# Threshold searches with TENSOR_TENSOR alone on GpSimd, looks over 583 columns, and searches in batches 2 to 5

## The chip, the cores and the metric

The kernel runs on one core of a Trainium2 chip. The metric is the device time of one execution in microseconds; smaller is better. The core's engines are named as in the profile: PE (matrix products), PEld (its weight loads), DVE (vector engine), ACT (scalar engine), POOL (GpSimd) and SP (which issues DMAs).

## The reference

Two stages follow each other: attention in which each query keeps its 32 largest scores, and a two-layer network with a squared ReLU.

```python
# q, k, v: (8 batches, 8 heads, 576 rows, 64), float32
scores = scale * np.matmul(q, k.transpose(0, 1, 3, 2))
kth = np.partition(scores, -32, axis=-1)[..., -32:-31]
scores = np.where(scores >= kth, scores, -1000000000.0)
scores = scores - np.max(scores, axis=-1, keepdims=True)
attn = np.exp(scores)
attn = attn / (np.sum(attn, axis=-1, keepdims=True) + 1e-09)
attn_out = np.matmul(attn, v)
# x: attn_out as (4608, 512); w_in (512, 2048), w_out (2048, 512)
h = x @ w_in
r = np.maximum(h, 0.0)
out = (r * r) @ w_out
```

## The kernel before

**Groups.** The 64 heads form 32 pairs. A group is 128 query rows of both heads of a pair, so a row of SBUF holds 2 x 576 scores. A pair has four and a half groups; the half ones (the last 64 rows, `Z` in the code) of two pairs make one group. That gives 144 groups, 18 in each batch.

**A usual group** (`top_k`, L820). PE makes the scores in PSUM, ACT copies them to a tile `s` (L752; there are five). The 32nd largest score of each row is then found on DVE: folds in PSUM make a quarter-size array of maxima (L890), POOL adds and subtracts scores as integers, which leaves the smaller partners (L885: two kinds of `u`, then `f`), and DVE takes the eight largest and strikes them out, in turn (L919, L924, L928, L931). With the threshold `kth`, ACT makes a mask `w` (L950, two instructions), PE transposes scores and mask, ACT takes the exponential (L1006), and PE multiplies with the values. Chunks of finished rows go through the network: ReLU on ACT (L1125), squares on POOL (L1137) or ACT (L1140), output copies on ACT (L1157), stores from SP.

**A hunted group.** Four groups find their threshold another way (`hunt`, L756, with `hunted`, L812, for the mask), with ACT and POOL in place of DVE. ACT copies the scores to the one tile `hs`. Then ACT *looks* at them six times, two instructions each (`look`, L766), into the one tile `hz`, with a sum per row as a by-product. The first look gives the sum of squares, from which POOL makes a first threshold (a scaling, then a power of 1/2, L778 and L779). Each of the next four looks takes the sign of threshold minus score; the sum tells how many scores lie above. POOL corrects the threshold in four small operations on two columns (`tiny`, L784 to L789): it rounds the count's distance from its aim to a multiple of 16 by adding and taking off a large constant (`ROUND`), multiplies by a gain and by the first threshold, and adds. The sixth look gives signs and a final count. POOL multiplies signs and scores (L793), so that the scores below the threshold are the largest, DVE takes their eight largest (L795), and POOL selects by the count which of the eight is the 32nd (L797, L799; `hot` holds the eight counts). DVE brings it into `hth` (L800). POOL compares it with 0 and with the last threshold and writes into `fcmp` (L803 to L807).

**Flag and second pass.** At the end (`verdict`, L1361) DVE reduces all comparisons of `fcmp` to one flag. If it is set, the program computes everything again with full searches on DVE. In the profiled execution it was not.

**Order of work.** There is no order by hand. Each operation is handed to a planner (`Plan.op`, L109) with an engine, an estimated duration, a priority and its dependencies; `Plan.schedule` (L141) runs the whole program through these estimates, takes on each engine the ready operation with the smallest priority, and what comes out is the fixed order on each engine's queue. On the chip, semaphores keep dependencies, and a queue waits in order. A group's priorities are counted from `tg = T0 + PER * (number of groups before)`, with PER = 5.3. In a search, look `j` has priority `tg + HO + HS * j`, its POOL operations `tg + HS * j - 14`, the two maxima `tg + HD`. HO, HS, HD are constants (L448), and `HA`, `HP`, `HZ` are estimates of durations.

**Where searches lie.** `HUNT` (L465) names the hunted groups, by batch, head pair and group, and how many groups earlier the search begins: `{(2, 2, 3): 12, (3, 2, 3): 12, (4, 2, 3): 12, (6, 2, 3): 12}`. In batches 5 and 6 the two half groups come first; in batch 6 the groups are ordered by rows ahead of head pairs, in batches 1 to 5 by head pairs.

**Setup.** `setup` (L1306) writes constants, with POOL's `hot` columns among them (L1323, L1324).

Of the kernel before, what the change touches and what calls it, by code (L numbers as in the profile page):

```python
# [6 lines left out]
ALU = mybir.AluOpType  # L7
ACTF = mybir.ActivationFunctionType
AX = mybir.AxisListType
FP32 = mybir.dt.float32  # L10
# [3 lines left out]
P = 128  # L14
TOPK = 32
NEG = -3.0e38
# [368 lines left out]
def bass_top_k_attn__then__act_relu_squared_kernel(  # L385
# [71 lines left out]
    NGRP = NALL // 2  # L457
    NF = 3
    GAP = QUART + NGRP // NF + 8
# [11 lines left out]
    hk = sb("hk", [P, NH, 2 * (NSTEP + 1) + 8 * NSTEP + 2 + 2 + 32 + 4])  # L471
# [9 lines left out]
    sizes = {  # L481
        "rq": ([P, 5, 2, D], FP32, 3), "rk": ([P, 5, 2, D], FP32, 2), "rv": ([P, 10, D], FP32, 2),
        "qk": ([P, 2 * S + 64], FP32, 5), "vb": ([P, 10, D + 1], BF16, 5),
        "s": ([P, 2 * S + 4], FP32, 5), "hs": ([P, 2, S], FP32, 1), "hz": ([P, 2 * S + 4], FP32, 1), "u": ([P, 2 * (HALF + QUART) + 4], FP32, 1), "f": ([P, 2, 2 * GAP + S + NGRP // NF], FP32, NF), "a": ([P, 2, 8], FP32, 2),
        "sh": ([P, 2], FP32, 2), "w": ([P, 2, S], BF16, 3), "p": ([P, 9, 128], BF16, 3),
        "av": ([P, 10, D + 1], FP32, 2), "x": ([P, 10, D], BF16, 3), "xt": ([P, NCT, 256], BF16, 3),
        "xz": ([P, NCT, 64 * 2], BF16, 2), "o": ([P, DM], FP32, 2),
# [1 line left out]
    mem = {nm: sb(nm, *spec) for nm, spec in sizes.items()}  # L489
# [17 lines left out]

    def at(t):
        x = mem[t.pool.name][t.slot]
        if t.pool.name == "hz":  # L510
            return x[:, 2:2 + 2 * S].rearrange("p (i c) -> p i c", i=2)
# [16 lines left out]
    act, vec, gp, pe = nc.scalar, nc.vector, nc.gpsimd, nc.tensor  # L528
# [57 lines left out]
    def build(full, weights, pl):  # L586
        state = {"h": 0, "n": 0, "u": 0, "pairs": 0, "last": {}}
        kths, rzs, checks, sought = [], [], [], {}
# [167 lines left out]
        def hunt(k, gi, qks, tg):  # L756

            st, hz = tile("hs"), tile("hz")
            score(gi, qks, tg, st)
            used = [0]  # L760

            def small(n_):
                used[0] += n_
                return lambda a=0, b=n_, c=used[0] - n_: hk[:, k, c + a:c + b]

            def look(j, func, acc, after, bias=None):  # L766
                kw = [dict() if bias is None else dict(bias=bias(i, i + 1), scale=-1.0) for i in range(2)]
                return [pl.op("act", HA - .09 * (j == 0), tg + HO + HS * j + .1 * i, lambda i=i: act.activation(  # L768
                    at(hz)[:, i, :], at(st)[:, i, :], func, accum_out=acc(i, i + 1), **kw[i]), r=[st], after=after,
                    w=[hz] if j == 0 else [], hold=[] if j == 0 else [hz], take=[hz] if j == i == 0 else [])  # L770
                    for i in range(2)]
# [4 lines left out]
            q, t0 = small(2), small(2)  # L776
# [3 lines left out]
            t = t0  # L780
            for j in range(NSTEP):
                a, r, v, m, t_ = small(2), small(2), small(2), small(2), small(2)
                got = look(j + 1, ACTF.Sign, a, got, t)
                got = tiny(j + 1, lambda a=a, r=r: gp.tensor_scalar(  # L784
                    r(), a(), 27.5 * 2 - S, ROUND, ALU.add, ALU.add), got)
                got = tiny(j + 1, lambda r=r, v=v, j=j: gp.tensor_scalar(
                    v(), r(), ROUND, -GAIN[j] / START / 2, ALU.subtract, ALU.mult), got)
                got = tiny(j + 1, lambda v=v, m=m: gp.tensor_tensor(m(), v(), t0(), ALU.mult), got, .155)
                got = tiny(j + 1, lambda t=t, m=m, t_=t_: gp.tensor_tensor(t_(), t(), m(), ALU.add), got, .155)  # L789
                t = t_  # L790
            a, z8, pick = small(2), small(16), small(16)
            got = look(NSTEP + 1, ACTF.Sign, a, got, t)
            z = pl.op("gp", HZ, tg + HS * (NSTEP + 1) - 14, lambda: gp.tensor_tensor(  # L793
                at(hz)[:, :, :], at(hz)[:, :, :], at(st)[:, :, :], ALU.mult), r=[st], hold=[hz], after=got)
            mx = [pl.op("dve", .065 + S / 960, tg + HD, lambda i=i: vec.max(z8(8 * i, 8 * i + 8), at(hz)[:, i, :]),  # L795
                        hold=[hz], after=[z]) for i in range(2)]
            which = [pl.op("gp", .26, tg + HS * (NSTEP + 1) - 13, lambda i=i: gp.tensor_scalar(  # L797
                pick(8 * i, 8 * i + 8), hot[:, 0:8], a(i, i + 1), None, ALU.is_equal), after=got + [hotted[0]]) for i in range(2)]
            got = tiny(NSTEP + 1, lambda: gp.tensor_tensor(pick(), pick(), z8(), ALU.mult), which + mx, .16)  # L799
            th = [pl.op("dve", .09, tg + HD, lambda: vec.tensor_reduce(  # L800
                hth[:, :, k:k + 1], pick().rearrange("p (i c) -> p i c", i=2), AX.X, ALU.max), after=got)]
            d, at_ = small(2), 2 * (NGRP - NH) + 4 * k
            o = tiny(NSTEP + 8, lambda: gp.tensor_scalar(  # L803
                fcmp[:, at_:at_ + 2], hth[:, :, k], 0.0, None, ALU.is_le), th)
            checks.extend(o)
            o = tiny(NSTEP + 8, lambda: gp.tensor_tensor(d(), hth[:, :, k], t(), ALU.subtract), th)
# [433 lines left out]
        for b in range(NB):  # L1240
            seq, stages = batch_order(b)
            pairs, held, got = {}, {}, {}
# [8 lines left out]
            for hp, gi, kind in plan_:  # L1251
                tg = T0 + PER * (state["n"] + HN * state["h"])
# [21 lines left out]
                r0, n_ = 128 * js[0], 128 * len(js) if gi != Z else 64  # L1274
                i, col = place(b, r0, n_)
# [28 lines left out]
    state_pre, hotted = [], []  # L1304

    def setup(pl):  # L1306
# [12 lines left out]
        h1 = pl.op("gp", .1, -96.9, lambda: gp.memset(heads[0:64, 0:1], 1.0), after=[h0, i2, i3, i4, i5])  # L1319
        h2 = pl.op("gp", .1, -96.8, lambda: gp.memset(heads[64:128, 1:2], 1.0), after=[h1])  # L1320
        x = h2
        for i in range(8):
            x = pl.op("gp", .1, 20 + i, lambda i=i: gp.memset(hot[:, i:i + 1], S - 2.0 * 31 + 2 * i), after=[x])  # L1323
# [11 lines left out]
        for i in range(16):  # L1335
            s = tile("ws")
# [12 lines left out]
            eng, fn = ("act", act.copy) if i % 4 < WA else ("gp", gp.tensor_copy)  # L1349
# [5 lines left out]
        for x, dur in times:  # L1355
            t = Tile(psum)
# [4 lines left out]
    def verdict(pl, kths, rzs, squared, place, masked, checks):  # L1361

        G = NGRP - NH
        free, t, at_ = place
        fc = fcmp[:, 0:2 * G].rearrange("p (l g) -> p l g", l=2)
        x = pl.op("dve", .4, 1e6, lambda: vec.tensor_tensor(fc, c16[:, :, 0:G], c24[:, :, 0:G], ALU.min), after=kths, order=masked)
# [125 lines left out]
```

## Time and profile before

| | |
|---|---|
| median of 3 runs | 778.52 us (778.34 to 780.71) |
| profiled execution: device time | 782.27 us |
| profiled execution: span from first to last instruction | 780.4 us |
| mean granted clock of PE | 0.993 |
| read from HBM, written | 36.70 MB, 9.44 MB |

Each row of a group view names the line, engine, operation, `out<-in`, the count, then the total busy time, the mean duration in ns, and the idle time of the engine before it with what ended that. A timeline row has start and duration in us ahead of the same names, and in brackets the idle time just before. Intervals of neighbours on one engine may overlap a little, so the distance of two starts says what an instruction takes of its queue.

### The profile page before, as it was taken

What the parts mean: (1) busy time and instruction counts of PE and PEld (TensorE: products, weight loads), DVE (VectorE), ACT (ScalarE), POOL (GpSimd) and SP (SyncE); (2) the same over time, 40 slices, a digit from 0 to 9 for tenths busy, and PEclk for the clock granted to TensorE, in tenths of its full rate; (3) what the DMA queues carried; (4) which work ended last, traced back from release to release, by engine and by line L of the source; (5) the groups of instructions that cost most, each with busy time, mean ns of one, the idle gap of its engine ahead of it and who ended that gap; (6) DMA issues with size and microseconds to landing.
All of it is one profiled execution on the core that took longest, in us unless ns stands there. A gap on an engine that the chain in (4) does not pass through costs nothing.

```text
span 780.4 us, 27779 instructions
## 1 busy us (share of the span) xinstructions
PE 707.9 (91%) x10632; PEld 531.7 (68%) x10705; DVE 751.9 (96%) x3584; ACT 718.2 (92%) x1140; POOL 693.1 (89%) x718
## 2 busy tenths in 40 slices
PE   7788888999889989988998989999899989999997
PEld 3656666666666676666776757776677777787776
DVE  5999999999999999999999999999999999999995
ACT  4798989899899999999999999998998999998884
POOL 3898998889789999998998999998898999999991
PEclk9999999999999999999999999999999999999999
DMA  8657452032400134104231034200441020110101
GB/s 189 169 143 198 112 147 56 23 82 49 111 11 10 50 82 95 32 21 101 62 85 38 3 91 90 67 7 22 103 107 54 16 73 22 34 27 22 34 25 34
DMA packets 144890, 52.65 MB, mean 67 GB/s; under 512 B 137072, under 2 KB 137072, under 8 KB 144752
## 3 DMA queue, kind: packets, MB, share of 16 engines
q1 hardware_dynamic: 144080, 50.66, 26.7%
q8 instruction: 85, 1.39, 0.8%
q14 instruction: 53, 0.43, 0.2%
q10 hardware_dynamic: 672, 0.16, 0.1%
HBM read 36.70 MB, written 9.44 MB: 59 GB/s over the span
## 4 chain that ended last, share of the span: by engine, by line
ACT 44%; DVE 22%; PE 22%; POOL 9%; issue 3%; DVEq 0%; POOLq 0%
PE ps L579 18%; ACT p L1006 10%; ACT w L950 9%; ACT s L752 9%; DVE f L928 7%; DVE f L890 5%; ACT g L1125 5%; DVE c L924 5%; PE ps L582 3%; POOL f L885 3%; POOL u L885 3%; DVE f L919 3%; ACT hz L768 3%; DVE kth L931 2%; ACT g L1140 2%
## 5 line engine op out<-in xcount | busy, mean ns | idle before, releaser
L885 POOL TENSOR_TENSOR f<-u,f 128x864 int32<-128x864 int32 x138 | 236.9, 1717 | 7.5
L950 ACT ACTIVATE w<-s,kth 128x576 bf16<-128x576 f32 x278 | 217.9, 822 | 4.8 <-DVE kth L931 4.5
L928 DVE MATCH_REPLACE8 f<-c,f 128x98 f32<-128x98 f32 (+2 forms) x840 | 221.3, 270 | 0.0
L924 DVE MAX8 c<-f 128x8 f32<-128x98 f32 (+2 forms) x840 | 201.3, 273 | 0.0
L579 PE MATMUL ps<-qk 64*128 64x384 f32 (+3 forms) x1280 | 181.5, 431 | 6.6 <-DVE f L890 5.3
L885 POOL TENSOR_TENSOR u<-f,s 128x576 int32<-128x576 int32 x138 | 166.8, 1209 | 18.2 <-DVE f L890 17.5
L1006 ACT ACTIVATE p<-ps 128x1152 bf16<-128x1152 f32 x144 | 168.2, 1168 | 11.5 <-PE ps L579 11.2
L752 ACT COPY s<-ps 128x1152 f32<-128x1152 f32 x140 | 161.0, 1150 | 18.2 <-PE ps L579 17.8
L579 PEld LDWEIGHTS ps<-qk 64*128 64x128 f32 (+1 forms) x1280 | 131.9, 177 | 40.5 <-DVE f L928 10.3
L579 PE MATMUL ps<-xt,win 128*128 128x256 bf16 (+1 forms) x1280 | 132.5, 252 | 9.0 <-ACT g L1125 2.7
L579 PE MATMUL ps<-wo,g 128*128 128x512 bf16 (+1 forms) x519 | 127.1, 373 | 13.0 <-issue 6.6
L885 POOL TENSOR_TENSOR u<-s 128x288 int32<-128x288 int32 x138 | 110.7, 802 | 24.2 <-ACT s L752 19.9
L890 DVE TENSOR_TENSOR f<-ps,f 128x288 f32<-128x288 f32 x280 | 123.8, 442 | 0.1
L931 DVE MAX8 kth<-f 128x8 f32<-128x296 f32 x280 | 122.1, 457 | 0.0
L579 PEld LDWEIGHTS ps<-xt,win 128*128 128x128 bf16 x1280 | 97.5, 98 | 29.6 <-ACT g L1125 5.2
L582 PEld LDWEIGHTS ps<-ident,s 64*128 64x128 f32 x2520 | 97.2, 140 | 29.9 <-ACT w L950 14.6
L919 DVE MAX8 f<-f 128x8 f32<-128x288 f32 x280 | 114.5, 448 | 0.0
L582 PE MATMUL ps<-ident,s 64*128 64x64 f32 x2520 | 107.4, 227 | 5.2 <-ACT w L950 4.8
L1137 POOL TENSOR_TENSOR g<-g 128x512 bf16<-128x512 bf16 x86 | 89.7, 1045 | 4.5 <-ACT g L1125 4.1
L1125 ACT ACTIVATE g<-ps 128x512 bf16<-128x512 f32 x140 | 85.8, 638 | 2.0 <-PE ps L579 1.8
L579 PEld LDWEIGHTS ps<-wo,g 128*128 128x128 bf16 x592 | 50.1, 98 | 54.8 <-issue 4.5
L579 PEld LDWEIGHTS ps<-vb,p 128*128 128x128 bf16 (+1 forms) x1600 | 54.7, 101 | 30.4 <-ACT g L1125 8.2
(105 smaller groups left out, 860.7 us busy)
## 6 DMA issues: line engine op xcount, KB each, us to landing
rv<-in_v_dram SPq DMA_DIRECT2D x64, 128.0 KB, 2.4
out_dram<-o SPq DMA_DIRECT2D x32, 256.0 KB, 2.2
rk<-in_k_dram SPq DMA_DIRECT2D x63, 128.0 KB, 2.5
rq<-in_q_dram SPq DMA_DIRECT2D x62, 128.0 KB, 2.5
g<-in_moe_w_in_dram SPq DMA_DIRECT2D x8, 512.0 KB, 4.3
g<-in_moe_w_out_dram SPq DMA_DIRECT2D x8, 512.0 KB, 4.3
rq<-in_q_dram SPq DMA_DIRECT2D x32, 32.0 KB, 2.6
rv<-in_v_dram SPq DMA_DIRECT2D x64, 16.0 KB, 2.2
```

Source lines behind the costliest of these rows:

```text
L579: return pe.matmul(o, l, r, start=start, stop=stop, skip_group_check=True)
L582: return pe.matmul(o, i, ident, is_transpose=True, skip_group_check=True, **kw)
L752: cp = [pl.op("act", 1.1, tg - LEAD + 1, lambda: act.copy(at(st)[:, :, 0:S], two(banks(ss)[:, FIRST_AT:], SECOND, S)), r=[ss], w=[st])]
L885: return pl.op("gp", dur, prio, lambda: gp.tensor_tensor(o().bitcast(I32), x().bitcast(I32), y().bitcast(I32), op), **kw)
L890: return dve(.36, lambda: vec.tensor_tensor(o(), two(banks(ss)[:, FIRST_AT + c:], SECOND, QUART), x(), ALU.max), r=[ss], **kw)
L919: prev[i] = [dve(.065 + HALF / 960, lambda i=i: vec.max(at(f)[:, i, A + 7:A - 1:-1], at(f)[:, i, M + QUART:E]), after=prev[i] + [low], hol ...
L924: lambda i=i, t=t, c0=c0, c1=c1: vec.max(eighth(t, i), at(f)[:, i, c0:c1]),
L928: lambda i=i, t=t, c0=c0, c1=c1: vec.match_replace(at(f)[:, i, c0:c1], eighth(t, i), at(f)[:, i, c0:c1], NEG), hold=[f])]
L931: ks.append(chain(kth, i, prev[i], .065 + (8 + HALF) / 960, lambda i=i: vec.max(eighth(kth, i), at(f)[:, i, A:M + QUART]), hold=[f]))
L950: masks[i:] = [pl.op("act", .77, tw + .8 * i, lambda i=i: act.activation(at(wt)[:, i, :], at(st)[:, i, 0:S], ACTF.Relu, bias=kth[:, i, n:n ...
L1006: return act.activation(at(pt)[:, :, :].rearrange("p c (h q) -> p h c q", h=2), bass.AP(x.tensor, x.offset, [x.ap[0], [APART, 2], [64, 9], ...
L1125: return act.activation(at(g)[:, 0:kf * nt], bank(hh)[:, 0:kf * nt], ACTF.Relu)
```

## The change

POOL's small operations all become TENSOR_TENSOR: what was an immediate number is now a pair of equal columns of `hot`, written once in setup. The first scaling is gone; instead the root is multiplied by ten columns in one operation (`ts`), which gives the first threshold and the four steps' gains. So that the sum `55 - 576` and `ROUND` make one constant that float32 holds exactly, the looks from the second on (five, two instructions each) read 583 columns: seven more, which lie before the first and behind the second half of `hs` and hold a large negative number. The selection by count is written with differences: the eight counts less the found one, both scaled by 2^53, squared, and subtracted from the eight scores. The comparisons with 0 and the last threshold leave POOL; `htt` collects the last thresholds, and `verdict` compares all four searches at once in four small DVE instructions. The tiles `hs` and `hz` get margins. The fourth search moves from batch 6 to batch 5, with a lead of 11 groups, and HS, HD and HO change.

```diff
-    HN, HA, HP, HZ, HS, HD, HO = .3, .86, .68, 2.18, 6, 40, 20
+    HN, HA, HP, HZ, HS, HD, HO = .3, .86, .68, 2.18, 5, 32, 22
...
-    HUNT = {(2, 2, 3): 12, (3, 2, 3): 12, (4, 2, 3): 12, (6, 2, 3): 12}
+    HUNT = {(2, 2, 3): 12, (3, 2, 3): 12, (4, 2, 3): 12, (5, 2, 3): 11}
...
-    START, ROUND = 1.66, 1.5 * 2.0 ** 27
+    START, ROUND, ODD, FAR = 1.66, 1.5 * 2.0 ** 27, 7, 2.0 ** 53
...
-    hot = sb("hot", [P, 10])
+    htt = sb("htt", [P, 2, NH])
+    fh = sb("fh", [P, 2, 2, NH])
+    hot = sb("hot", [P, 18 + 2 * NSTEP])
...
+            def wider(t, i, more):
+                x = mem[t.pool.name][t.slot]
+                c = 8 if t.pool.name == "hs" else 10
+                return x[:, c + S * i - ODD * (more and i == 0):c + S * i + S + ODD * (more and i == 1)]
...
             def look(j, func, acc, after, bias=None):
...
-                    at(hz)[:, i, :], at(st)[:, i, :], func, accum_out=acc(i, i + 1), **kw[i]), r=[st], after=after,
+                    wider(hz, i, j > 0), wider(st, i, j > 0), func, accum_out=acc(i, i + 1), **kw[i]),
+                    r=[st], after=after,
...
-            def tiny(j, fn, after, dur=.19, **kw):
-                return [pl.op("gp", dur, tg + HS * j - 14, fn, after=after, **kw)]
+            def tiny(j, o, x, y, op, after, dur=.155):
+                return [pl.op("gp", dur, tg + HS * j - 14, lambda: gp.tensor_tensor(o(), x(), y(), op), after=after)]
...
-            got = tiny(0, lambda: gp.tensor_scalar(q(), q(), START ** 2 / S, None, ALU.mult), got)
-            got = tiny(0, lambda: gp.tensor_tensor(t0(), q(), hot[:, 8:10], ALU.pow), got + [hotted[0]], HP)
+            got = tiny(0, root, q, fixed(0), ALU.pow, got + [hotted[0]], HP)
+            got = tiny(0, rows(ts, 2), spread(root), lambda: hot[:, 16:18 + 2 * NSTEP].rearrange("p (i c) -> p i c", c=2), ALU.mult, got)
...
-                got = tiny(j + 1, lambda a=a, r=r: gp.tensor_scalar(
-                    r(), a(), 27.5 * 2 - S, ROUND, ALU.add, ALU.add), got)
-                got = tiny(j + 1, lambda r=r, v=v, j=j: gp.tensor_scalar(
-                    v(), r(), ROUND, -GAIN[j] / START / 2, ALU.subtract, ALU.mult), got)
-                got = tiny(j + 1, lambda v=v, m=m: gp.tensor_tensor(m(), v(), t0(), ALU.mult), got, .155)
-                got = tiny(j + 1, lambda t=t, m=m, t_=t_: gp.tensor_tensor(t_(), t(), m(), ALU.add), got, .155)
+                got = tiny(j + 1, r, a, fixed(1), ALU.add, got)
+                got = tiny(j + 1, v, r, fixed(2), ALU.subtract, got)
+                got = tiny(j + 1, m, v, gain, ALU.mult, got)
+                got = tiny(j + 1, t_, t, m, ALU.add, got)
...
-            which = [pl.op("gp", .26, tg + HS * (NSTEP + 1) - 13, lambda i=i: gp.tensor_scalar(
-                pick(8 * i, 8 * i + 8), hot[:, 0:8], a(i, i + 1), None, ALU.is_equal), after=got + [hotted[0]]) for i in range(2)]
-            got = tiny(NSTEP + 1, lambda: gp.tensor_tensor(pick(), pick(), z8(), ALU.mult), which + mx, .16)
+            got = tiny(NSTEP + 1, big, a, fixed(3), ALU.mult, got)
+            got = tiny(NSTEP + 1, rows(far), lambda: hot[:, 0:8].unsqueeze(1).broadcast_to([P, 2, 8]),
+                       lambda: big().unsqueeze(2).broadcast_to([P, 2, 8]), ALU.subtract, got, .165)
+            got = tiny(NSTEP + 1, wide, far, far, ALU.mult, got, .165)
+            got = tiny(NSTEP + 1, pick, z8, wide, ALU.subtract, got + mx, .165)
...
-            o = tiny(NSTEP + 8, lambda: gp.tensor_scalar(
-                fcmp[:, at_:at_ + 2], hth[:, :, k], 0.0, None, ALU.is_le), th)
-            checks.extend(o)
-            o = tiny(NSTEP + 8, lambda: gp.tensor_tensor(d(), hth[:, :, k], t(), ALU.subtract), th)
-            checks.extend(tiny(NSTEP + 8, lambda: gp.tensor_scalar(
-                fcmp[:, at_ + 2:at_ + 4], d(), 0.0, None, ALU.is_ge), o))
+            checks.extend(th)
...
-        for i in range(8):
-            x = pl.op("gp", .1, 20 + i, lambda i=i: gp.memset(hot[:, i:i + 1], S - 2.0 * 31 + 2 * i), after=[x])
-        hotted.append(pl.op("gp", .1, 28, lambda: gp.memset(hot[:, 8:10], 0.5), after=[x]))
+        at_start = START / S ** .5
+        marks = [(8, 10, .5), (10, 12, ROUND + 27.5 * 2 - S - ODD), (12, 14, ROUND), (14, 16, FAR), (16, 18, at_start)]
+        marks += [(18 + 2 * i, 20 + 2 * i, -x_ / 2 / S ** .5) for i, x_ in enumerate(GAIN)]
+        marks += [(i, i + 1, FAR * (S + ODD - 2.0 * 31 + 2 * i)) for i in range(8)]
+        for i, (c0, c1, x_) in enumerate(marks):
+            x = pl.op("gp", .1, 20 + i, lambda c0=c0, c1=c1, x_=x_: gp.memset(hot[:, c0:c1], x_), after=[x])
+        for c in (8 - ODD, 8 + 2 * S):
+            x = pl.op("gp", .1, 38, lambda c=c: gp.memset(mem["hs"][0][:, c:c + ODD], NEG), after=[x])
+        hotted.append(x)
...
-        ends = [pl.op("dve", .35, 1e6, lambda: vec.tensor_reduce(fone[:, 0:1], fcmp[:, 0:2 * G + 4 * NH], AX.X, ALU.max), after=done + checks)]
+        flat = lambda x: x.rearrange("p l k -> p (l k)")
+        y = pl.op("dve", .1, 1e6, lambda: vec.tensor_scalar(
+            fcmp[:, 2 * G:2 * G + 2 * NH], flat(hth[:, :, :]), 0.0, None, ALU.is_le), after=checks)
+        x = pl.op("dve", .1, 1e6, lambda: vec.tensor_scalar(fh[:, 0, :, :], htt[:, :, :], 1e18, None, ALU.min), after=checks)
+        x = pl.op("dve", .1, 1e6, lambda: vec.tensor_tensor(fh[:, 1, :, :], fh[:, 0, :, :], hth[:, :, :], ALU.is_gt), after=[x])
+        x = pl.op("dve", .1, 1e6, lambda: vec.tensor_scalar(
+            fcmp[:, 2 * G + 2 * NH:2 * G + 4 * NH], flat(fh[:, 1, :, :]), 0.5, None, ALU.is_lt), after=[x])
+        ends = [pl.op("dve", .35, 1e6, lambda: vec.tensor_reduce(fone[:, 0:1], fcmp[:, 0:2 * G + 4 * NH], AX.X, ALU.max), after=done + [x, y])]
```

More of the change, by code (lines that the diff above doesn't have):

```diff
@@ L468, in bass_top_k_attn__then__act_relu_squared_kernel @@
     GAIN = (.014, .008, .005, .003)
-    START, ROUND = 1.66, 1.5 * 2.0 ** 27
+    START, ROUND, ODD, FAR = 1.66, 1.5 * 2.0 ** 27, 7, 2.0 ** 53
     fcmp = sb("fcmp", [P, NALL + 4 * NH])
-    hk = sb("hk", [P, NH, 2 * (NSTEP + 1) + 8 * NSTEP + 2 + 2 + 32 + 4])
+    hk = sb("hk", [P, NH, 12 * NSTEP + 4 + 6 + 64])
     hth = sb("hth", [P, 2, NH])
-    hot = sb("hot", [P, 10])
+    htt = sb("htt", [P, 2, NH])
+    fh = sb("fh", [P, 2, 2, NH])
+    hot = sb("hot", [P, 18 + 2 * NSTEP])
     fone = sb("fone", [P, 8])
@@ L483, in bass_top_k_attn__then__act_relu_squared_kernel @@
         "qk": ([P, 2 * S + 64], FP32, 5), "vb": ([P, 10, D + 1], BF16, 5),
-        "s": ([P, 2 * S + 4], FP32, 5), "hs": ([P, 2, S], FP32, 1), "hz": ([P, 2 * S + 4], FP32, 1), "u": ([P, 2 * (HALF + QUART) + 4], FP32, 1), "f": ([P, 2, 2 * GAP + S + NGRP // NF], FP32, NF), "a": ([P, 2, 8], FP32, 2),
+        "s": ([P, 2 * S + 4], FP32, 5), "hs": ([P, 2 * S + 16], FP32, 1), "hz": ([P, 2 * S + 20], FP32, 1), "u": ([P, 2 * (HALF + QUART) + 4], FP32, 1), "f": ([P, 2, 2 * GAP + S + NGRP // NF], FP32, NF), "a": ([P, 2, 8], FP32, 2),
         "sh": ([P, 2], FP32, 2), "w": ([P, 2, S], BF16, 3), "p": ([P, 9, 128], BF16, 3),
@@ L509, in at @@
         x = mem[t.pool.name][t.slot]
-        if t.pool.name == "hz":
-            return x[:, 2:2 + 2 * S].rearrange("p (i c) -> p i c", i=2)
+        if t.pool.name in ("hs", "hz"):
+            c = 8 if t.pool.name == "hs" else 10
+            return x[:, c:c + 2 * S].rearrange("p (i c) -> p i c", i=2)
         if t.pool.name in ("s", "u"):
@@ L764, in small @@
                 return lambda a=0, b=n_, c=used[0] - n_: hk[:, k, c + a:c + b]
+            def wider(t, i, more):
+                x = mem[t.pool.name][t.slot]
+                c = 8 if t.pool.name == "hs" else 10
+                return x[:, c + S * i - ODD * (more and i == 0):c + S * i + S + ODD * (more and i == 1)]
             def look(j, func, acc, after, bias=None):
@@ L776, in hunt, with fixed, spread, rows @@
-            q, t0 = small(2), small(2)
+            def tiny(j, o, x, y, op, after, dur=.155):
+                return [pl.op("gp", dur, tg + HS * j - 14, lambda: gp.tensor_tensor(o(), x(), y(), op), after=after)]
+            def fixed(i):
+                return lambda: hot[:, 8 + 2 * i:10 + 2 * i]
+            def spread(x):
+                return lambda: x().unsqueeze(1).broadcast_to([P, NSTEP + 1, 2])
+            def rows(x, n_=8):
+                return lambda: x().rearrange("p (i c) -> p i c", c=n_)
@@ L777, in hunt @@
+            q, root, ts = small(2), small(2), small(2 * NSTEP + 2)
             got = look(0, ACTF.Square, q, [])
-            got = tiny(0, lambda: gp.tensor_scalar(q(), q(), START ** 2 / S, None, ALU.mult), got)
-            got = tiny(0, lambda: gp.tensor_tensor(t0(), q(), hot[:, 8:10], ALU.pow), got + [hotted[0]], HP)
-            t = t0
+            got = tiny(0, root, q, fixed(0), ALU.pow, got + [hotted[0]], HP)
+            got = tiny(0, rows(ts, 2), spread(root), lambda: hot[:, 16:18 + 2 * NSTEP].rearrange("p (i c) -> p i c", c=2), ALU.mult, got)
@@ L781, in hunt @@
+            t = lambda a=0, b=2: ts(a, b)
             for j in range(NSTEP):
                 a, r, v, m, t_ = small(2), small(2), small(2), small(2), small(2)
+                gain = lambda j=j: ts(2 * j + 2, 2 * j + 4)
+                if j == NSTEP - 1:
+                    t_ = lambda a=0, b=2: htt[:, a:b, k]
                 got = look(j + 1, ACTF.Sign, a, got, t)
-                got = tiny(j + 1, lambda a=a, r=r: gp.tensor_scalar(
-                    r(), a(), 27.5 * 2 - S, ROUND, ALU.add, ALU.add), got)
@@ L790, in hunt @@
+                got = tiny(j + 1, m, v, gain, ALU.mult, got)
+                got = tiny(j + 1, t_, t, m, ALU.add, got)
                 t = t_
-            a, z8, pick = small(2), small(16), small(16)
+            a, big, far, wide, z8, pick = small(2), small(2), small(16), small(16), small(16), small(16)
             got = look(NSTEP + 1, ACTF.Sign, a, got, t)
             z = pl.op("gp", HZ, tg + HS * (NSTEP + 1) - 14, lambda: gp.tensor_tensor(
-                at(hz)[:, :, :], at(hz)[:, :, :], at(st)[:, :, :], ALU.mult), r=[st], hold=[hz], after=got)
@@ L795, in hunt @@
-            mx = [pl.op("dve", .065 + S / 960, tg + HD, lambda i=i: vec.max(z8(8 * i, 8 * i + 8), at(hz)[:, i, :]),
+                at(hz)[:, :, 0:S], at(hz)[:, :, 0:S], at(st)[:, :, 0:S], ALU.mult), r=[st], hold=[hz], after=got)
+            mx = [pl.op("dve", .065 + S / 960, tg + HD, lambda i=i: vec.max(z8(8 * i, 8 * i + 8), at(hz)[:, i, 0:S]),
                         hold=[hz], after=[z]) for i in range(2)]
-            which = [pl.op("gp", .26, tg + HS * (NSTEP + 1) - 13, lambda i=i: gp.tensor_scalar(
-                pick(8 * i, 8 * i + 8), hot[:, 0:8], a(i, i + 1), None, ALU.is_equal), after=got + [hotted[0]]) for i in range(2)]
@@ L800, in hunt @@
             th = [pl.op("dve", .09, tg + HD, lambda: vec.tensor_reduce(
                 hth[:, :, k:k + 1], pick().rearrange("p (i c) -> p i c", i=2), AX.X, ALU.max), after=got)]
-            d, at_ = small(2), 2 * (NGRP - NH) + 4 * k
-            o = tiny(NSTEP + 8, lambda: gp.tensor_scalar(
-                fcmp[:, at_:at_ + 2], hth[:, :, k], 0.0, None, ALU.is_le), th)
-            checks.extend(o)
-            o = tiny(NSTEP + 8, lambda: gp.tensor_tensor(d(), hth[:, :, k], t(), ALU.subtract), th)
```

## The prediction

> **What bounds the kernel now.** I read the page's first lines, then the busy time by stretch, then VectorE's waits.
>
> ```profile
> span 780.4 us, 27779 instructions
> PE 707.9 (91%) x10632; PEld 531.7 (68%) x10705; DVE 751.9 (96%) x3584; ACT 718.2 (92%) x1140; POOL 693.1 (89%) x718
> ```
>
> VectorE (DVE) has 28.5 us without work in 780.4. The columns of the next view are: stretch, length, then busy time of PE, PEld, DVE, ACT and POOL, each with its instructions.
>
> ```profile
> 20.00:80.00 60.00, 48.71 (x740) 37.32 (x741) 58.97 (x283) 51.85 (x76) 51.59 (x46) 0.97 0.66 165
> 80.00:200.00 120.00, 108.13 (x1603) 78.84 (x1612) 119.86 (x577) 109.72 (x167) 109.22 (x96) 1.00 0.33 81
> 204.00:297.00 93.00, 83.35 (x1254) 63.47 (x1259) 92.12 (x442) 91.71 (x152) 84.93 (x93) 1.00 0.21 46
> 297.00:390.00 93.00, 84.54 (x1281) 62.86 (x1284) 90.74 (x431) 92.16 (x151) 87.31 (x96) 1.00 0.27 64
> 390.00:470.00 80.00, 73.26 (x1048) 54.83 (x1056) 78.01 (x372) 77.91 (x130) 73.99 (x82) 0.96 0.23 57
> 470.00:580.00 110.00, 104.27 (x1654) 79.48 (x1664) 108.05 (x521) 103.06 (x159) 100.51 (x91) 1.00 0.28 65
> 580.00:676.00 96.00, 88.73 (x1331) 67.62 (x1341) 94.48 (x451) 93.95 (x161) 89.47 (x99) 1.00 0.16 41
> 700.00:760.00 60.00, 57.87 (x937) 44.98 (x943) 60.00 (x291) 52.20 (x77) 58.20 (x55) 1.00 0.10 27
> 760.00:780.00 20.00, 16.33 (x242) 12.80 (x242) 10.97 (x48) 9.50 (x19) 4.19 (x5) 1.00 0.10 34
> ```
>
> I chose the cuts so that one search lies in each of 204:297, 297:390, 390:470 and 580:676, and none in 470:580. Where no search has begun (80:200) DVE is idle for 0.14 us of 120, and after the last one (700:760) for none of 60. In between it loses 0.88, 2.26, 1.99, 1.95 and 1.52 us, together 8.6 of 472. In the four stretches with a search ACT too is full: 91.71 of 93, 92.16 of 93, 77.91 of 80, 93.95 of 96. So DVE sets the pace, with ACT beside it wherever a search runs; POOL has 2 to 9 us to spare in each. The change leaves the same 140 groups on DVE, so it can only move the 8.6 us and the ends of the kernel.
>
> ```profile
> DVE f L890 <- ACT s L752: 6.9, 12, 2.6
> DVE f L928 <- POOL f L885: 4.4, 9, 1.7
> DVE rzall L1054 <- PE ps L579: 2.7, 1, 2.7
> DVE hk L795 <- POOL hz L793: 0.2, 1, 0.2
> ```
>
> The waits (total, times, longest) name the two sources: score copies that come late from ACT (6.9 us, with one of 2.6 in it), and the integer subtraction `f` that comes late from POOL (4.4 us).
>
> **The change part by part.** First, the forms of instruction on POOL (count | busy us, mean ns):
>
> ```profile
> L786 POOL TENSOR_SCALAR hk<-hk 128x2 f32<-128x2 f32 x16 | 3.8, 237 | 1.3
> L784 POOL TENSOR_SCALAR hk<-hk 128x2 f32<-128x2 f32 x16 | 3.8, 237 | 2.7 <-ACT hz L768 1.4
> L788 POOL TENSOR_TENSOR hk<-hk 128x2 f32<-128x2 f32 x16 | 3.1, 196 | 0.5
> L797 POOL TENSOR_SCALAR hk<-hot,hk 128x8 f32<-128x8 f32 x8 | 2.5, 317 | 0.0
> L803 POOL TENSOR_SCALAR fcmp<-hth 128x2 f32<-128x2 f32 x4 | 0.9, 230 | 0.0
> L799 POOL TENSOR_TENSOR hk<-hk 128x16 f32<-128x16 f32 x4 | 0.9, 228 | 0.0
> L806 POOL TENSOR_TENSOR hk<-hth,hk 128x2 f32<-128x2 f32 x4 | 0.8, 197 | 0.0
> ```
>
> Removed: 32 TENSOR_SCALAR of the steps (7.6 us), the eight of L797 (2.5), the checks L803, L806 and L807 and the first scaling L778 (0.9 + 0.8, and twice 0.9 by L803's row). That is 13.5 us. Added: 32 TENSOR_TENSOR at 196 ns (6.3), four that spread the start over ten elements and four for `big` (between 196 and 228 ns, 1.7), eight for `far` and `wide` at L799's 228 ns (1.8). That is 9.8 us. Net 3.7 us of POOL time less, 0.9 a search. By the distance from one start to the next it is more:
>
> ```profile
> 382.27 0.23 POOL L803 TENSOR_SCALAR fcmp<-hth 128x2 f32<-128x2 f32 x1
> 382.46 0.20 POOL L806 TENSOR_TENSOR hk<-hth,hk 128x2 f32<-128x2 f32 x1
> 382.61 1.72 POOL L885 TENSOR_TENSOR f<-u,f 128x864 int32<-128x864 int32 x1
> ...
> 452.39 0.24 POOL L786 TENSOR_SCALAR hk<-hk 128x2 f32<-128x2 f32 x1
> 452.71 0.20 POOL L788 TENSOR_TENSOR hk<-hk 128x2 f32<-128x2 f32 x1
> 452.86 0.80 POOL L885 TENSOR_TENSOR u<-s 128x288 int32<-128x288 int32 x1
> ```
>
> In the last three rows the TENSOR_SCALAR holds the queue for 0.32 us and the TENSOR_TENSOR for 0.15; 32 times the difference is 5.4 us. It matters only where DVE waits for POOL. The longest such wait ended with the `f` of the third row:
>
> ```profile
> 384.36 0.09 DVE L928 MATCH_VALUE_LOAD f<-c,f 128x8 f32 x1 [1.71 <-POOL f L885]
> ```
>
> Of its 1.71 us, 0.34 (382.27 to 382.61) went to the two checks that the change takes off POOL. Bounds of the whole term: 0 (POOL had time to spare) and -4.4 us (every wait for POOL `f` goes). I take -0.7: these 0.34 us, and as much again over the eight other waits.
>
> The GPSIMD Engine Reference of the Trainium skill, section "Engine selection", speaks against this part: it calls two-input elementwise work on GpSimd about twice as slow as on VectorE, and one-input work roughly at line rate. If a TENSOR_TENSOR cost twice a TENSOR_SCALAR, the 32 swapped ones would add 32 x 0.237 = 7.6 us to POOL, and with the same share reaching DVE (0.7 of 3.7) this term would be +1.4 and the sum -0.4, 778.1 us. The rows of this case say the opposite at two elements, 196 against 237 ns, so I go by the rows.
>
> Second, the looks on ACT:
>
> ```profile
> L768 ACT ACTIVATE hz<-hs,hk 128x576 f32<-128x576 f32 x40 | 33.2, 832 | 1.6 <-POOL hk L789 1.4
> 390.00:470.00 80.00, 1.41 (x2) 10.54 (x24) 2.23 (x1) 0.96 0.23 57
> 580.00:676.00 96.00, 1.40 (x2) 11.31 (x24) 2.23 (x1) 1.00 0.16 41
> ```
>
> Seven columns more on 40 looks: at most 832/576 = 1.44 ns a column, 0.4 us in all, at least nothing. ACT is full around them, yet one full engine hands only part to the other; I take +0.1. ACT also waited 1.4 us, in three places, for the last small POOL operation of a step, with the score copies, masks and exponentials queued behind the look. Shorter steps take some of that away, and looks due every 5 us and starting 2 us later change the order on ACT. Bounds: -1.4 (all of it) and +1.4 (looks that come sooner push as many copies back); I take -0.7, nearer the gain, since every step does get shorter.
>
> Third, the fourth search moves from batch 6 to batch 5. The 12 looks of a search hold ACT for 10.5 to 11.3 us (the last two rows, of the tile `hz` alone: DVE, ACT, POOL). Stretch 580:676 loses that, and its 1.52 us of DVE idle should come near the 0.14 in 120 of a stretch without searches; I leave it 0.3 and take -1.2 (bounds -1.5 and 0). Stretch 470:580 gets it. That stretch already idles 1.95 us; the three earlier search stretches idle 0.88 to 2.26. I take 0 (bounds -1.1 and +0.3; ACT running over is a rival below). No load moves ahead with it: in batches 5 and 6 alike the 64-row groups come first, and their loads of this head pair stand before the search on SP's queue.
>
> The lead of 11 in place of 12 groups brings the reader of the threshold 5.4 us closer (751.9 us over 140 groups). The narrowest spare time now is in this same search:
>
> ```profile
> 666.18 0.15 DVE L800 TENSOR_REDUCE hth<-hk 128x2 f32<-128x16 f32 x1
> 670.89 1.54 ACT L815 ACTIVATE w<-hs,hth 128x576 bf16<-128x576 f32 x2
> ```
>
> It is 670.89 - 666.33 = 4.6 us. The last look comes due 3 us earlier (22 + 5x5 against 20 + 6x5), so 2.2 us are left and I take 0. The threshold's two maxima, now due at 32, were started as soon as their product was there (0.2 us of waiting for it), so their earlier due time also is worth 0.
>
> Fourth, the ends. Ten more memsets at the start (0.15 us each by the first row below), and four check instructions on DVE at the end (some 0.17 us each, as the last two rows):
>
> ```profile
> 5.02 1.21 POOL L1323 MEMSET hot<- 128x1 f32 x8
> 14.69 1.02 POOL L712 CAST vb<-rv 128x640 bf16<-128x640 f32 x1 [6.48 <-DMA rv<-in_v_dram]
> 765.14 0.17 DVE L1079 RECIPROCAL rzall<-av 128x2 f32<-128x2 f32 x1 [0.45 <-ACT av L1072]
> 768.00 0.17 DVE L1054 RECIPROCAL rzall<-ps 128x2 f32<-128x2 f32 x1 [2.69 <-PE ps L579]
> ```
>
> The memsets' 1.5 us lie in the 6.48 us that POOL waits for a load; uncovered, they would cost 1.5. The four check instructions wait only for thresholds that are over 100 us old by then, so they fit the 2.69 us that DVE waits for PE; without that cover they cost 0.7. I take 0 for both.
>
> Sum: -0.7 + 0.1 - 0.7 - 1.2 = -2.5 us. The profiled execution took 782.27 us, 1.87 more than its span, and would take 779.8; it lies 3.75 us above the median of the runs, so the forecast is 778.52 - 2.5 = **776.0 us**.
>
> **The rivals.** *ACT becomes the bound in batch 5.* Stretch 470:580 has 6.94 us of ACT time free and gets 10.5 to 11.3 us of looks: 3.6 to 4.4 us over. The decisive point is whether DVE can borrow from the stretch after; the score buffers are five, so only a few groups. For it: in every search stretch ACT is within 2.1 us of full, and now four follow each other without a rest. Against it: the same imbalance in 297:390 cost DVE 2.26 us, and the hunted group spares DVE 3.8 us there (5.4 less some 1.6 for its maxima, 1.4 of it in the rows of `hz`). If the overrun stays and the other terms give -0.7, the time is 778.5 + 4.0 - 0.7 = 781.8 us.
>
> *Nearly all stalls go.* With 8.6 us at stake and both sources relieved, DVE could run as in 80:200. All of it gone gives 769.9 us; if the 3.75 us by which the profiled run exceeds the median are such stalls, only 4.9 are there, 773.6. I put this case at 772.
>
> *The gain is hidden anyway.* POOL is not the bound, ACT's load is the same, and the stall in 580:676 reappears in 470:580: 0 to -1, 778.0 us. Likewise if a different order puts other operations in front of `f`.
>
> *The change does not do what it says:* a search that misses its window sets the flag and everything is computed again, at least another 780 us. The rounding steps work on the same multiples of 16 (576 + 7 - 55 = 528), so I give it under 0.01.
>
> **How the numbers follow.** Forecast 0.45 (own range 774.0 to 777.8), ACT overrun 0.25, hidden 0.18, nearly all stalls gone 0.12. A measurement of this kernel tells about 0.3%, 2.3 us, from no change: the bounds are 776.2 and 780.9. Of the forecast, 0.31 lies below 776.2 and 0.14 above; with 0.12 that is 0.43 faster. Same: 0.14, 0.15 of the hidden case and 0.02 of the overrun, 0.31. Slower: 0.23 and 0.03, 0.26. The range 771.0 to 782.5 leaves out the bottom of the third rival and the top of the first, about 0.15.
>
> **What would show it.** POOL's small operations all near 0.2 us, its busy time down by some 4 us; DVE idle below 0.5 us in the batch without a search and near 2 in batch 5; DVE's waits for POOL `f` below 4.4 us; the time between threshold and its reader above zero in all four searches. I am wrong if DVE waits for score copies in batch 5 grow by more than 2 us (the overrun), or if the total of DVE's idle time between 204 and 676 us stays within 1 us of 8.6.

## The result, and the profile after

| | before | after |
|---|---|---|
| median of 22 runs each, us | 780.1 (777.22 to 782.87) | 776.66 (775.67 to 779.3) |
| span of the profiled execution, us | 780.4 | 774.7 |

The ratio is 0.9961, with a 95% interval of 0.9949 to 0.9972: 3.0 us faster where 2.5 were forecast. The size came out, but in good part by luck: of the three terms that made it, the experiments bear out the rewrite alone.

Part of the difference goes with PE's granted clock: of 79 runs of the kernel before that were taken beside the experiments, the 20 at a mean clock of 0.993 or less have a median of 782.1 us and the 32 at 0.998 or more one of 778.3, and the changed kernel was at 0.998 or more in 21 of its 22 runs (median 776.65). A straight line through the times and clocks of these 101 runs leaves the changed kernel 1.6 us faster at an equal clock (an estimate). Whether the new order also brings the higher clock is not shown. The profiled execution of before was at 0.993, so the two profiles lie 5.7 us apart, further than the medians.

Busy time by stretch of the changed kernel, with the cuts of before (stretch, length, then PE, PEld, DVE, ACT, POOL):

```profile
20.00:80.00 60.00, 49.87 (x774) 38.26 (x767) 59.72 (x287) 53.18 (x80) 53.60 (x47) 0.97 0.66 169
204.00:297.00 93.00, 84.09 (x1268) 63.76 (x1275) 92.15 (x438) 91.77 (x151) 84.90 (x92) 1.00 0.20 46
297.00:390.00 93.00, 83.72 (x1303) 63.50 (x1310) 92.72 (x442) 92.83 (x154) 87.77 (x96) 1.00 0.27 64
390.00:470.00 80.00, 73.67 (x1103) 54.85 (x1111) 79.47 (x379) 79.49 (x134) 74.09 (x82) 1.00 0.25 62
470.00:580.00 110.00, 102.62 (x1573) 78.67 (x1580) 106.77 (x509) 110.00 (x182) 102.72 (x110) 1.00 0.25 58
580.00:676.00 96.00, 91.61 (x1471) 71.40 (x1480) 95.86 (x467) 90.43 (x145) 88.00 (x82) 1.00 0.17 44
```

DVE's idle time between 204 and 676 us fell from 8.6 to 0.85 + 0.28 + 0.53 + 3.23 + 0.14 = 5.0 us. The gain lies in 297:470, where 4.25 us became 0.81, and in 580:676, now without a search. But 470:580, which has the fourth search now, went from 1.95 to 3.23, and ACT is busy there for 110.00 of 110 us. The stretch 20:80 lies before the first search and gained 0.75 us; a2 below, whose engine queues there are those of the kernel before, is idle for 0.27 us there, so single executions differ by as much.

DVE's waits in the changed kernel (total, times, longest):

```profile
DVE f L905 <- ACT s L755: 3.5, 5, 2.6
DVE f L943 <- POOL f L900: 2.8, 2, 1.9
DVE rzall L1069 <- PE ps L582: 1.8, 1, 1.8
```

Late score copies fell from 6.9 to 3.5 us, late `f` from 4.4 to 2.8. POOL's groups:

```profile
L783 POOL TENSOR_TENSOR hk<-hk,hot 128x2 f32<-128x2 f32 x40 | 9.8, 246 | 1.4 <-ACT hz L776 1.0
L783 POOL TENSOR_TENSOR hk<-hk 128x2 f32<-128x2 f32 x28 | 5.5, 196 | 0.9
L783 POOL TENSOR_TENSOR hk<-hk 128x16 f32<-128x16 f32 x8 | 1.7, 212 | 0.0
L783 POOL TENSOR_TENSOR hk<-hk,hot 128x10 f32<-128x10 f32 x4 | 0.8, 208 | 0.0
```

The first row holds the four powers too, which took 722 ns each before; without them it comes to (9.8 - 2.9) / 36 = 0.19 us. On the page POOL's busy time fell from 693.1 to 687.4 us.

### The profile page after: what moved, and what is told of

Read it like the earlier page. It is cut to its first block, busy times and chain, and to the rows that moved or that the text cites. A ratio compares the mean times of both kernels' runs of the same rounds, so it can differ in the third digit from the quotient of the medians.

```text
span 774.7 us, 27736 instructions
## 1 busy us (share of the span) xinstructions
PE 703.3 (91%) x10608; PEld 528.1 (68%) x10679; DVE 751.1 (97%) x3588; ACT 717.9 (93%) x1140; POOL 687.4 (89%) x720
## 4 chain that ended last, share of the span: by engine, by line
ACT 58%; PE 20%; DVE 15%; POOL 4%; issue 3%; POOLq 0%; DVEq 0%; ACTq 0%
PE ps L582 16%; ACT w L965 13%; ACT p L1021 12%; ACT s L755 11%; ACT g L1140 7%; DVE f L943 4%; ACT hz L776 4%; DVE f L905 3%; PE ps L585 3%; DVE c L939 3%; ACT g L1155 3%; DVE f L934 2%; DVE kth L946 2%; POOL u L900 2%; ACT av L1087 2%
## 5 line engine op out<-in xcount | busy, mean ns | idle before, releaser
L965 ACT ACTIVATE w<-s,kth 128x576 bf16<-128x576 f32 x278 | 220.4, 830 | 3.5 <-DVE kth L946 3.5
L582 PE MATMUL ps<-qk 64*128 64x384 f32 (+3 forms) x1280 | 179.6, 427 | 6.6 <-DVE f L905 5.6
L582 PEld LDWEIGHTS ps<-vb,p 128*128 128x128 bf16 (+1 forms) x1600 | 54.0, 100 | 32.7 <-ACT g L1140 10.5
```

Of the source, the lines that this page charges most:

```text
L582: return pe.matmul(o, l, r, start=start, stop=stop, skip_group_check=True)
L965: masks[i:] = [pl.op("act", .77, tw + .8 * i, lambda i=i: act.activation(at(wt)[:, i, :], at(st)[:, i, 0:S], ACTF.Relu, bias=kth[:, i, n:n ...
```

## The experiments

Ratios are to the kernel before, run beside each, with 95% intervals. Two theories stood against each other. "Terms": each part has a worth of its own, as in the prediction, and the parts add. "Order": what counts is which fixed order the planner finds.

**One part, or two, at a time.** a1: the search alone is moved.

```diff
-    HUNT = {(2, 2, 3): 12, (3, 2, 3): 12, (4, 2, 3): 12, (6, 2, 3): 12}
+    HUNT = {(2, 2, 3): 12, (3, 2, 3): 12, (4, 2, 3): 12, (5, 2, 3): 11}
```

> The kernel before with only the fourth search moved to batch 5, lead 11; POOL's operations and the due dates as before. Theory 'terms' (each part is worth its own term, and they add): -1.2 us, ratio 0.9985, with DVE's idle time in 580:676 down to 0.3 us. Rival 'order' (what counts is which order the planner happens to find, the parts have no worth of their own): anything between 0.996 and 1.006, no relation to the term. Rival 'overrun' (ACT becomes the bound in batch 5): +3 us, 1.004, with ACT at 110 of 110 us in the stretch 470:580 and more DVE idle time there than the 1.95 us of before.

Measured: 1.0060 (1.0035 to 1.0085). a2: the due dates alone.

```diff
-    HN, HA, HP, HZ, HS, HD, HO = .3, .86, .68, 2.18, 6, 40, 20
+    HN, HA, HP, HZ, HS, HD, HO = .3, .86, .68, 2.18, 5, 32, 22
```

> The kernel before with only the due dates changed (HS 5, HD 32, HO 22). Theory 'terms': -0.7 us, 0.9991, hardly to be told from 1. Rival 'order': between 0.996 and 1.006. If due dates alone make the change, 0.996.

Measured: 1.0064 (1.0040 to 1.0087). a3: the rewrite alone, so the changed kernel with both lines put back.

> The changed kernel with the searches and due dates of before: TENSOR_TENSOR alone, 583 columns, checks once on DVE. Theory 'terms': -0.6 us, 0.9992, and POOL's small operations 3.7 us cheaper in sum. Rival 'order': between 0.996 and 1.006. If the rewrite alone makes the change, 0.996.

Measured: 1.0074 (1.0053 to 1.0095). a4: both lines, without the rewrite.

> The kernel before with search and due dates as in the changed kernel, TENSOR_SCALAR and the checks left on POOL: the changed kernel without the rewrite. Theory 'terms': -1.9 us, 0.9976. Rival 'order': no sum of the two parts alone. If the rewrite is what counts, 1.000.

Measured: 1.0047 (1.0034 to 1.0059). b1 and b2 are the changed kernel with one of the two lines put back (the first, then the second).

> The changed kernel with its fourth search put back into batch 6, lead 12. Theory 'terms': 1.2 us slower than the changed kernel, 0.9976 of before (changed: 0.9961). Rival 'order': between 0.994 and 1.004, with no relation to that.

> The changed kernel with the due dates of before (HS 6, HD 40, HO 20). Theory 'terms': 0.7 us slower than the changed kernel, 0.997 of before. Rival 'order': between 0.994 and 1.004.

Measured: 1.0071 (1.0051 to 1.0092) and 1.0070 (1.0044 to 1.0097). Every part alone, and every pair of parts, is slower than both kernels. The terms do not add.

**The same work in another order.** b4 moves a due date by 0.4 us.

```diff
-    HN, HA, HP, HZ, HS, HD, HO = .3, .86, .68, 2.18, 5, 32, 22
+    HN, HA, HP, HZ, HS, HD, HO = .3, .86, .68, 2.18, 5, 32, 22.4
```

> The changed kernel with the looks due 0.4 us later (HO 22.4 for 22), which takes nothing away and adds nothing: another order with the same work. Theory 'terms': 0.9961, as the changed kernel, within 0.0015. Rival 'order': a shift as large as those of the parts, 0.002 or more from 0.9961.

Measured: 1.0069 (1.0043 to 1.0094), 1.1% above the changed kernel. All six runs were at a granted clock of 0.993; at an equal clock some 0.7% are left (an estimate by straight lines as above). c1 changes two estimates in the kernel before.

```diff
-            def tiny(j, fn, after, dur=.19, **kw):
+            def tiny(j, fn, after, dur=.32, **kw):
...
-            which = [pl.op("gp", .26, tg + HS * (NSTEP + 1) - 13, lambda i=i: gp.tensor_scalar(
+            which = [pl.op("gp", .32, tg + HS * (NSTEP + 1) - 13, lambda i=i: gp.tensor_scalar(
```

> The kernel before, with the planner's estimate for POOL's small TENSOR_SCALAR raised from 0.19 us (0.26 for the selection) to the 0.32 us that they hold POOL's queue; the instructions are the same. Theory that the rewrite helps because the planner no longer underrates POOL: faster, 0.998, with DVE's waits for POOL f under 3 us (4.4 before). Rival, that only POOL's time itself counts: 1.000. Rival 'order': anything between 0.996 and 1.006.

Measured: 1.0077 (1.0051 to 1.0103), with DVE's waits for POOL `f` at 6.6 us. Truer estimates did not help. So an order alone is worth about 1%, and more than the whole change at an equal clock too.

**The order held, the instructions exchanged.** d1 has the changed kernel's order on every queue, with 32 TENSOR_SCALAR back in it.

```diff
+            def scalar(j, fn, after):
+                return [pl.op("gp", .155, tg + HS * j - 14, fn, after=after)]
...
-                got = tiny(j + 1, r, a, fixed(1), ALU.add, got)
-                got = tiny(j + 1, v, r, fixed(2), ALU.subtract, got)
+                got = scalar(j + 1, lambda a=a, r=r: gp.tensor_scalar(r(), a(), 27.5 * 2 - S - ODD, ROUND, ALU.add, ALU.add), got)
+                got = scalar(j + 1, lambda r=r, v=v: gp.tensor_scalar(v(), r(), ROUND, None, ALU.subtract), got)
```

> The changed kernel with the 32 rounding operations of the steps as TENSOR_SCALAR again, on the same data, while the planner still takes them for 0.155 us, so that the order on every queue is that of the changed kernel, instruction for instruction. Theory 'order' (the order alone makes the change): 0.996, as the changed kernel (0.9961). Theory 'terms' (0.7 us for the cheaper operations): 0.997. If POOL's time were on the path in full, 32 x 0.17 = 5.4 us more: 1.003.

d3 is the reverse: the order of before, with the steps in TENSOR_TENSOR.

```diff
+            def first(j, r, a):
...
+                return gp.tensor_tensor(r(), a(), hot[:, 10:12], ALU.add)
...
-                got = tiny(j + 1, lambda a=a, r=r: gp.tensor_scalar(
-                    r(), a(), 27.5 * 2 - S, ROUND, ALU.add, ALU.add), got)
-                got = tiny(j + 1, lambda r=r, v=v, j=j: gp.tensor_scalar(
-                    v(), r(), ROUND, -GAIN[j] / START / 2, ALU.subtract, ALU.mult), got)
+                got = tiny(j + 1, lambda a=a, r=r, j=j: first(j, r, a), got)
+                got = tiny(j + 1, lambda r=r, v=v: gp.tensor_tensor(v(), r(), hot[:, 12:14], ALU.subtract), got)
...
```

> The kernel before, in its own order on every queue, with the steps' 32 TENSOR_SCALAR replaced by TENSOR_TENSOR and the looks over 583 columns; the planner keeps its old estimates; four small operations more, one a search. The selection and the checks stay as they were. Theory 'order': 1.000. Theory 'terms': 0.9993 (some 0.5 us). If POOL's time were on the path in full: 0.993.

Measured: d1 0.9975 (0.9958 to 0.9991), d3 0.9958 (0.9938 to 0.9978). In the order of before, the exchange in the steps, with the looks over 583 columns, is worth 0.42%, 3.3 us (1.7 to 4.8), by the ratio. Part of this goes with the clock: a straight line through the runs of both kernels leaves 2.0 us at an equal clock (an estimate, 0.8 either way), and the medians of the runs at 0.998 or more (seven of d3, ten of before) differ by 0.7. Nor does the profile show where the gain lies: DVE's idle time from 204 to 676 us is 8.3 us in d3 and 8.6 in before. So the exchange makes the kernel faster, but its worth is open between 0.7 and 3.3 us. In the changed kernel's order its undoing costs 0.9975 - 0.9961 = 0.14%, 1.1 us, and the two intervals overlap. The instructions of d1:

```profile
L808 POOL TENSOR_SCALAR hk<-hk 128x2 f32<-128x2 f32 x16 | 3.8, 236 | 2.1 <-ACT hz L776 1.0
L809 POOL TENSOR_SCALAR hk<-hk 128x2 f32<-128x2 f32 x16 | 3.6, 224 | 1.3
```

and those in their place in d3, both at 196 ns:

```profile
L792 POOL TENSOR_TENSOR hk<-hk,hot 128x2 f32<-128x2 f32 x16 | 3.1, 196 | 2.1 <-ACT hz L774 1.7
L798 POOL TENSOR_TENSOR hk<-hk,hot 128x2 f32<-128x2 f32 x16 | 3.1, 196 | 0.4
```

**Which order is good?** While it makes the order, the planner also gets an estimate of the end of the program (`span`, L1403 before). e1 and f1 were picked by it. e1:

```diff
-    HN, HA, HP, HZ, HS, HD, HO = .3, .86, .68, 2.18, 5, 32, 22
+    HN, HA, HP, HZ, HS, HD, HO = .25, .86, .68, 2.18, 5.2, 34, 18
...
-    HUNT = {(2, 2, 3): 12, (3, 2, 3): 12, (4, 2, 3): 12, (5, 2, 3): 11}
+    HUNT = {(2, 2, 3): 12, (3, 2, 3): 12, (4, 2, 3): 12, (5, 2, 3): 10}
```

and f1:

```diff
-    LEAD = 40
+    LEAD = 40.8
...
-    MQ = 19.61
+    MQ = 19.59
...
-    ML = 12
+    ML = 11.6
...
-    TA = 7.2
+    TA = 7.6
...
-    HN, HA, HP, HZ, HS, HD, HO = .3, .86, .68, 2.18, 5, 32, 22
+    HN, HA, HP, HZ, HS, HD, HO = .3, .86, .68, 2.18, 4.8, 28, 21
```

> The changed kernel with quite other due dates (HN 0.25, HS 5.2, HD 34, HO 18, the last lead 10): the same work in another order, picked because the planner's own estimate of the end is low for it, 772.5 in the planner's time. That estimate is 771.3 for the changed kernel, 771.9 for the one before, and 774.4 to 778.3 for the eight variants so far, which all ran at 1.005 to 1.008. Theory 'the planner's estimate ranks the orders': 0.997 to 1.000. Rival 'the chip's own waits decide and the estimate says nothing': 1.0064, the mean of the eight, with 1.005 as the lower end. Theory 'terms': 0.996, since nothing of the rewrite or of the move is undone.

> The changed kernel with other due dates (HS 4.8, HD 28, HO 21, and LEAD 40.8, MQ 19.59, ML 11.6, TA 7.6 for the usual groups): the same work in another order, for which the planner's own estimate of the end is 771.3, the same as for the changed kernel. Theory 'the planner's estimate ranks the orders': 0.996, within 0.002, and if its DVE waits are no longer, a second order as good as the changed kernel's. Rival 'the changed kernel's order is one lucky order on the chip': 1.003 or more, toward the 1.0064 of the eight variants with late estimates.

Measured: e1 0.9980 (0.9962 to 0.9997), f1 0.9962 (0.9944 to 0.9979). (The mean of the eight variants is 1.0067, not the 1.0064 of the two expectations.) All kernels, sorted by the planner's estimate; the last two columns are DVE's idle time in two stretches, length less busy time of the view by stretch:

```
kernel    planned end   ratio    470:580  580:676   fourth search in
changed   771.3         0.9961   3.23     0.14      batch 5
f1        771.3         0.9962   2.90     0.28      batch 5
d1        771.3         0.9975   4.88     0.15      batch 5
before    771.9         1        1.95     1.52      batch 6
d3        771.9         0.9958   1.40     1.58      batch 6
e1        772.5         0.9980   4.19     0.35      batch 5
a1        774.4         1.0060   3.91     0.43      batch 5
a4        774.8         1.0047   3.14     0.71      batch 5
b4        776.6         1.0069   6.26     0.17      batch 5
a3        776.8         1.0074   1.63     0.79      batch 6
b1        777.0         1.0071   1.49     4.06      batch 6
b2        777.0         1.0070   4.42     0.07      batch 5
c1        777.6         1.0077   1.88     1.91      batch 6
a2        778.3         1.0064   0.40     1.75      batch 6
```

All six kernels with an estimate up to 772.5 ran at or below the time of before, and all eight from 774.4 on at 1.0047 or more. Both forecasts made from the estimate held, f1 against the rival by a wide margin. But d1 has the changed kernel's order and d3 that of before, so these are four orders, and only e1 and f1 were picked by the estimate before they ran. Inside the late group all intervals overlap, so whether it ranks those kernels cannot be told (c1's estimate, besides, counts longer durations), and it cannot see what d3 gained, since the planner kept its old durations there.

## Why the prediction was right, and where it was not

*What bounds the kernel.* Right: DVE's 8.6 us of idle time around the searches were the place. They fell by 3.6 in the profile, and the time by 3.0 by the ratio. But this idle time does not rank the kernels: a3 and b1 idle for 6.0 and 7.3 us there, less than before, and ran 0.7% slower; in a3 more idle time after 676 us (11.8 against 9.7) and 1.7 us more of DVE's own busy time show in the profile. The 3.75 us by which the profiled execution lay above the median, which the prediction thought might be stalls, are about what lies between runs at a clock of 0.993 or less and those at 0.998 or more (782.1 against 778.3).

*The rewrite, -0.7 us.* The direction was right. Where it could be measured with the order held, it is worth 0.7 to 3.3 us in the order of before, by how the clock is counted, and 1.1 in the changed order; all of it lies in the prediction's bounds (0 to -4.4), and 0.7 is the lower end. POOL's operations cost what the rows said. The exchange also shortens steps that ACT waits for, which the prediction had put into the next term; how much came by which way stays open. The prediction had set against this part what the Trainium skill, page "GPSIMD Engine Reference", section "Engine selection", says of two-input work. That section compares GpSimd with VectorE and not the two forms on GpSimd. Here, at two columns, the two-input form is the cheaper, 196 against 224 to 237 ns, and going back to the other form (d1) did not make the kernel faster.

*Shorter steps and due dates, -0.7 us.* Not shown. Alone the due dates cost 0.64% (a2), a shift of 0.4 us in one of them 1.1% (b4 against the changed kernel), and f1 has other ones and the same time. The due dates have no worth of their own that shows; they choose the order.

*The move, -1.2 us.* This step failed: "Stretch 470:580 gets it. ... I take 0". The relief in 580:676 came as forecast, 0.14 us left where 0.3 were. But in all eight kernels with the search in batch 5, 470:580 idles 2.90 to 6.26 us, on average 4.1; in the six with batch 6 it is 1.5. The averages of 580:676 are 0.3 and 1.9. By these averages, which go over different orders, the move costs the two stretches about 1.0 us (4.4 against 3.4) where it was to save 1.2; from before to the changed kernel they come out even (3.47 and 3.37). The first rival, ACT becoming the bound in batch 5, had a part of the mechanism: ACT is at 110.00 of 110 us in the changed kernel and in f1. It came at a third of its price (1.3 of 3.6 to 4.4 us), and not by the way that the prediction named, late score copies at DVE: those waits fell in 470:580 from 1.2 to 0.2 us. What grew there are DVE's waits for POOL `f`, from 0.9 to 2.8 us, in two places. The longer one goes back to ACT through POOL, which had itself waited for a score copy (first POOL's row, then DVE's):

```profile
493.38 0.80 POOL L900 TENSOR_TENSOR u<-s 128x288 int32<-128x288 int32 x1 [1.84 <-ACT s L755]
498.38 0.09 DVE L943 MATCH_VALUE_LOAD f<-c,f 128x8 f32 x1 [1.93 <-POOL f L900]
```

Ahead of the other, 0.86 us, POOL had no pause: `f` stood behind POOL's own work. d3 comes to the changed kernel's ratio with the search left in batch 6.

*What I had left out of the sum.* A change of priorities does not add terms to the order that is there; it makes the planner find another. I had that as half a sentence in the rival "the gain is hidden" and gave it 0 to -1 us. The runs put 0.5 to 0.7% on it for the parts and pairs of parts. The changed kernel escapes it: for all three parts together the planner's estimate comes out low again, at 771.3. That the total met the forecast is luck as far as it rests on this. Why an order with a late estimate also loses time on the chip is not shown.

*The ends.* The memsets were hidden, as forecast: POOL's wait for the load behind them fell from 6.48 to 5.02 us. The four checks took 0.15 to 0.18 us each in the changed kernel, as priced, but not in every order (below). *The lead of 11* left 8.1 us to spare in the fourth search, more than the 2.2 worked out, and the other three have 8.2 to 10.8:

```profile
556.72 0.16 DVE L821 TENSOR_REDUCE hth<-hk 128x2 f32<-128x16 f32 x1
...
564.98 0.89 ACT L830 ACTIVATE w<-hs,hth 128x576 bf16<-128x576 f32 x1
```

Two slips in the working did not matter: the operations removed from POOL add up to 13.6 us by their rows, not 13.5, and in the four stretches with a search POOL had 5.7 to 8.1 us to spare, not 2 to 9.

## What to carry to other kernels

Where a planner fixes the order, hold the order and exchange the instructions to learn what an instruction is worth; a part undone through the planner measures another order, here worth up to 1.1%. After any edit it is worth choosing the due dates anew by the planner's own end before measuring, as the two orders picked so here suggest; an edit that looks slower by half a per cent may only have lost its order. Compare runs at an equal granted clock before a gain of a few tenths of a per cent is put down to the edit. A heavy side task moved into a stretch must be priced on the engine that runs it there: 11.6 us of looks (10.5 to 11.3 were expected) into 6.9 us of free time on ACT gave back to DVE what the old place released.

## What was not expected of the hardware

In b1 two of the four checks, which take 0.15 to 0.18 us in the changed kernel, came while POOL was at work. First DVE, then POOL:

```profile
756.80 1.17 DVE L1394 TENSOR_SCALAR fcmp<-hth 128x8 f32<-128x8 f32 x1
757.89 1.08 DVE L1396 TENSOR_SCALAR fh<-htt 128x8 f32<-128x8 f32 x1
759.00 0.17 DVE L1397 TENSOR_TENSOR fh<-fh,hth 128x8 f32<-128x8 f32 x1
759.21 0.17 DVE L1398 TENSOR_SCALAR fcmp<-fh 128x8 f32<-128x8 f32 x1
```

```profile
756.23 1.71 POOL L900 TENSOR_TENSOR f<-u,f 128x864 int32<-128x864 int32 x1
757.90 1.04 POOL L1152 TENSOR_TENSOR g<-g 128x512 bf16<-128x512 bf16 x1
```

The first check ends at 757.97 and POOL's `f` at 757.94; the second ends at 758.97 and POOL's square at 758.94. Eight columns on DVE waited for the rest of POOL's instruction the first time, and for the whole of it the second. In a3 one check took 1.76 us, and it too ended 0.03 us after POOL's `f`; in b4 a check that began 0.05 us before POOL's square took its usual 0.17. The Trainium skill, page "SBUF — State Buffer", section "Who interferes with whom", says that a `tensor_scalar` on DVE can take a pair of ports that it shares with GpSimd, and that whichever is issued first holds the pair for its whole instruction while the other is blocked. The rows of b1 agree to 0.03 us; which of the two was issued first they do not show for the second check. The prediction priced the checks by rows that POOL did not disturb; in b1 the four took 2.6 us (1.17, 1.08 and twice 0.17), not 0.7.
